# Transposing DMAs in place of TensorE transposes for the rows of the expert blocks

## The chip, the cores and the metric

The kernel runs on one core of a Trainium2 chip. The metric is the device time of one execution in microseconds (us); lower is better. Engine names follow the profile: PE is TensorE (matrix products and transposes; PEld is its loading of weights), DVE is VectorE, ACT is ScalarE, POOL is GpSimd, SP is SyncE, which computes nothing and issues most of the DMAs. SPq is the queue of instructions of SyncE that issue DMAs.

## The reference

Two layers follow each other. The first is sparse attention over 4 batches with 8 heads, 768 positions and 64 elements per head: keys lie in chunks of 32, each query keeps the six chunks with the highest upper bound of its score, and softmax attention runs over these. Its output, seen as 3072 tokens of 512 elements, goes into a mixture of experts with a dense branch:

```
h_dense = np.maximum(x @ w1_dense, 0.0)
y_dense = h_dense @ w2_dense
logits = x @ w_gate
expert_idx = np.argmax(logits, axis=1)
...
    h = np.maximum(x[mask] @ w1[e], 0.0)
    y_moe[mask] = gate_w[mask, None] * (h @ w2[e])
return (y_dense + y_moe).astype(np.float32)
```

There are 8 experts, each with two 512 by 512 matrices; a token goes to one expert only. `gate_w` is the softmax weight of that expert.

## The kernel before, in words

**Attention, and the dense branch beside it.** The kernel works through 16 pairs of heads (four pairs per batch). While it works on the attention of one batch, the dense branch of the batch before is put in as filler: transposes of x (L257), the gate (L265 to L282), the dense products (L383, L392) and the stores of the dense result (L398, through SyncE's queue, two stores of 64 rows for each 128 tokens).

**The table.** Each token's attention output, in half precision, is kept as one row of 512 elements with 32 further 16-bit words, of which the first two are the gate weight (a float) and the next two the token's number (an integer). When the expert of a token is known, GpSimd scatters its row into `table` in device memory (L368), in which each expert has a range of rows. A row is 544 words of 16 bits, 1088 bytes. So the rows of one expert lie one behind the other, and a block is 128 such rows.

**The blocks.** There are at most 31 blocks of 128 rows; 28 run always, and the last three only if they are needed, behind a branch. The numbers of first row and of expert of each block are calculated on DVE and read into registers (L430). The first 11 blocks (`N1`) hold only tokens of the first three batches, and can be fetched while the last batch is still in its attention. The other 17 have to wait until the last batch's rows are in the table; the rows behind each expert's last token are filled with an empty pattern by eight DMAs (`empty`, L728 in the profile), which also precede them.

**One block.** `fetch(i)` (L448 to L452) puts one plain DMA into SyncE's queue, which brings the 128 rows into the tile `xg`, 128 partitions by 544 words. `tx(i)` transposes the 512 elements on TensorE, in four pieces of 128 by 128, into PSUM (L684), and DVE copies the result to `exT` (L686). `e1(i)` multiplies by the expert's first matrix (L692, four matmuls of 512 columns), ACT applies the relu (L695, tile `eh`). `th(i)` transposes this on TensorE (L701), ACT copies it to `ehT` (L703). `e2(i)` multiplies by the second matrix (L709), DVE multiplies by the gate weight, which is read from `xg` (L712, tile `yo`, four buffers), and GpSimd scatters the result into the output with an adding DMA (L713), by the token numbers, which are also read from `xg`.

**Order.** Each engine runs its instructions in the order in which they were put in its queue. The loop at the end puts, for each i, e1(i), tx(i+1), some pieces of the last batch's gate and dense branch in the first iterations, e2(i-1) and th(i). The loop puts in fetches up to 8 blocks ahead (`AHEAD`); the first six (`FIRST`) are put in already during the last pair of heads. A framework orders the queues by priority and adds the waits. `xg` has 14 buffers, so a fetch waits for a buffer only from the 15th block on. The DMAs of SyncE's queue use eight semaphores in turn, and each DMA waits for the one that used the same semaphore before, so that at most eight are under way.

Of the kernel before, what the change touches and what calls it, by code (L numbers as in the profile page):

```python
# [8 lines left out]
FP = mybir.dt.float32  # L9
BF = mybir.dt.bfloat16  # L10
HF = mybir.dt.float16
AF = mybir.ActivationFunctionType
ALU = mybir.AluOpType
# [4 lines left out]
def kernel(  # L18
# [12 lines left out]
    nc = tc.nc  # L31
# [3 lines left out]
    N, Dm = out.shape  # L35
    E = 8
    F = 512
    NK = Dm // 128
# [5 lines left out]
    XW = Dm + 32  # L44
    U16 = mybir.dt.uint16
# [8 lines left out]
    table = dram.tile([EMPTY + 128, XW], U16, name="table")  # L54
# [17 lines left out]
    eg = ctx.enter_context(tc.tile_pool(name="eg", bufs=14))  # L72
# [25 lines left out]
    ident = const.tile([128, 128], HF)  # L98
# [142 lines left out]
    def apart(dma, group, reason):  # L241

        if group in groups:
            tc.declare_no_dep(dma.ins, group=group, reason=reason)
        groups.add(group)
        tc.add_to_no_dep_group(group, dma.ins)
# [179 lines left out]
    offs = []  # L426
    rows = []
# [7 lines left out]
    def load_offs():  # L435

        k = len(offs)
        n, c = (min(4, N1 - k), k) if k < N1 else (min(4, NBLK - k), k - N1 + N1R)
        offs.extend(registers(eo[:, c : c + n], mybir.EngineType.PE, (E - 1) * 2 * NK * 512,
                              "the expert of a block is at most the last"))  # L440

    def load_rows(n):
        rows.extend(registers(ro[:, len(rows) : n], mybir.EngineType.SP, EMPTY,
                              "blocks lie in their expert's rows, or are the empty one"))

    es = [dict() for _ in range(NBLK)]

    def fetch(i):  # L448
        es[i]["x"] = xg = eg.tile([128, XW], U16, name="xg")
        ld = nc.sync.dma_start(out=xg, in_=table[bass.ds(rows[i], 128)])  # L450
        if i < N1:
            tc.add_to_no_dep_group("full", ld.ins)  # L452

    FIRST = 6
    with (
# [167 lines left out]
        for i, (p, u) in enumerate(seq):  # L623
# [37 lines left out]
            if p == NP - 1 and 3 <= u < 3 + FIRST:  # L661
                fetch(u - 3)
# [5 lines left out]
    with (  # L668
        tc.tile_pool(name="p1", bufs=2, space=bass.MemoryType.PSUM) as p1,
        tc.tile_pool(name="p2", bufs=2, space=bass.MemoryType.PSUM) as p2,  # L670
        tc.tile_pool(name="p3", bufs=2, space=bass.MemoryType.PSUM) as p3,
        tc.tile_pool(name="p4", bufs=1, space=bass.MemoryType.PSUM) as p4,
        tc.tile_pool(name="et", bufs=2) as et,
    ):
        cur.update(tr=(p1, "tr"), h=(p2, "h"), y=(p3, "y"), rk=(p4, "rk"))
        assert not fills
        a, d, ranks, places, _ = batch_fills(B - 1)

        wef = we.rearrange("p e j f -> p (e j f)")
        def tx(i):  # L680
            s = es[i]
            tp = p1.tile([128, NK, 128], HF, name="tp", tag="tr")
            for ko in range(NK):
                nc.tensor.transpose(tp[:, ko], s["x"][:, ko * 128 : (ko + 1) * 128].bitcast(HF), ident)  # L684
            s["xT"] = xT = et.tile([128, NK, 128], HF, name="exT")
            nc.vector.tensor_copy(xT, tp)  # L686

        def e1(i):
            s = es[i]
            hp = p2.tile([128, 512], FP, name="hp", tag="h")  # L690
            for ko in range(NK):
                nc.tensor.matmul(hp, s["xT"][:, ko], wef[:, bass.ds(offs[i] + ko * 512, 512)],  # L692
                                 start=(ko == 0), stop=(ko == NK - 1))
            s["h"] = h = et.tile([128, 512], HF, name="eh")
            nc.scalar.activation(h, hp, AF.Relu)  # L695

        def th(i):
            s = es[i]
            tp = p1.tile([128, NK, 128], HF, name="tp", tag="tr")
            for j in range(NK):  # L700
                nc.tensor.transpose(tp[:, j], s["h"][:, j * 128 : (j + 1) * 128], ident)  # L701
            s["hT"] = hT = et.tile([128, NK, 128], HF, name="ehT")
            nc.scalar.copy(hT, tp)  # L703

        def e2(i):
            s = es[i]
            yp = p3.tile([128, Dm], FP, name="yp", tag="y")
            for j in range(NK):
                nc.tensor.matmul(yp, s["hT"][:, j], wef[:, bass.ds(offs[i] + (NK + j) * 512, 512)],  # L709
                                 start=(j == 0), stop=(j == NK - 1))  # L710
            o = et.tile([128, Dm], FP, name="yo", bufs=4)
            nc.vector.tensor_scalar(o, yp, s["x"][:, Dm : Dm + 2].bitcast(FP), None, ALU.mult)  # L712
            sc = nc.gpsimd.indirect_dma_start(  # L713
                out=out, out_offset=bass.IndirectOffsetOnAxis(ap=s["x"][:, Dm + 2 : Dm + 4].bitcast(mybir.dt.int32), axis=0),
                in_=o, in_offset=None, bounds_check=N - 1, oob_is_err=False, compute_op=ALU.add)
            latest["pool"] = sc
            apart(sc, "add", "every token is in one block")
            if i < N1:
                tc.declare_no_dep(sc.ins, group="dense", reason="the first blocks hold no token of the last batch")
                tc.add_to_no_dep_group("add1", sc.ins)  # L720

        def empty():

            _, at_ = nc.values_load_multi_w_load_instructions(
                zo, engines=[mybir.EngineType.SP], min_val=0, max_val=EMPTY - 128,
                skip_runtime_bounds_check_because="an expert has room for all tokens and a block more")
            for e in range(E):
                z = nc.sync.dma_start(out=table[bass.ds(at_[e], 128)], in_=zt)  # L728
                apart(z, "rows", "these rows are no token's")
                tc.declare_no_dep(z.ins, group="full", reason="the first blocks end before these rows")  # L730

        AHEAD = 8
        READY = 4
        tx(0)
        extra = {0: a[:NT] + [a[NT], ranks], 1: places[:2], 2: places[2:4], 3: places[4:] + [empty]}
        for n, f in enumerate(d):
            extra.setdefault(1 + n * (N1 - 2) // len(d), []).append(f)
        got = FIRST

        RARE = 3  # L740
        NOFT = NBLK - RARE
        for i in range(NOFT):
            if i == READY:
                load_rows(NBLK)
            while got < min(i + AHEAD + 1, NOFT if i >= READY else N1):
                fetch(got)
                got += 1
            e1(i)
            if i + 1 < NOFT:
                tx(i + 1)  # L750
            for f in extra.get(i, ()):
                f()
            if i > 0:
                e2(i - 1)
            if len(offs) < min(i + 4, NBLK):
                load_offs()
            if i == READY + 1:
                total = nc.values_load(nblk, min_val=0, max_val=N2,  # L758
                                       skip_runtime_bounds_check_because="the blocks that are left are at most N2")
            th(i)  # L760
        e2(NOFT - 1)
        with tc.If(total > N2 - RARE):
            for i in range(NOFT, NBLK):
                fetch(i)
                tx(i)
                e1(i)
                th(i)
                e2(i)
# [30 lines left out]
```

## Time and profile before

| | |
|---|---|
| Median of the runs | 259.3 us (259.21 and 259.4) |
| The profiled execution | 258.3 us, its span 256.5 us |
| PE busy | 213.9 us (83%), 2547 instructions |
| DVE, ACT, POOL busy | 181.2, 177.7, 161.5 us |
| Transposes of x (L684) | 112, 219 ns each |
| Copies to exT (L686) | 28, 425 ns each |
| Row fetches (L450 in SyncE's queue) | 28, 136 KB each, 338 ns of the queue each (median) |
| Scatters into the output (L713) | 28, 1554 ns of POOL each, 5.1 us to landing |
| First and last scatter into the output start | 182.5 and 249.6 us |

The span is the time from the first to the last instruction of the profiled execution, and the execution's own time is a little longer. Busy time of an engine counts neither the issue of DMAs from SyncE nor waits. In the timeline, a line has the start in us from the beginning of the span, the duration (from the first to the last of a group where several are put together), engine, line, operation, the tile written and the tiles read, the number of instructions, and in brackets how long the engine was idle before it and what ended that. The expert loop runs from 173 us to the end; before it, nothing is touched by the change.

### The profile page before, as it was taken

Reading aid. Unit: us, or ns where it says so; the run is one execution under the profiler, and the core shown is the slowest. Engines: PE = TensorE matmul, PEld = TensorE weight load, DVE = VectorE, ACT = ScalarE, POOL = GpSimd, SP = SyncE. Lnnn points to the kernel's source line nnn. Section 1 sums busy time; section 2 is a strip of 40 time slices with the busy share of each in tenths; the row PEclk is TensorE's granted clock in tenths of the full one; section 3 lists DMA queues with packets and bytes.
Section 4 is the critical chain, followed back from the end, with each engine's and each line's share of the span. In section 5 each row is a group of like instructions: output and inputs, shape, how many; then the busy total and the mean of one; then the engine's idle time right before and its main releaser. Section 6 shows DMA issues by size and latency. Waiting matters only on the chain. (4 is left out here: it accounts for less than half of the span.)

```text
span 256.5 us, 7304 instructions
## 1 busy us (share of the span) xinstructions
PE 213.9 (83%) x2547; PEld 142.2 (55%) x2547; DVE 181.2 (71%) x622; ACT 177.7 (69%) x331; POOL 161.5 (63%) x197
## 2 busy tenths in 40 slices
PE   0379787787899798899996989979999999999960
PEld 0256565575666576656664766646555555555520
DVE  6878899999968699985799997236633345455440
ACT  2689897887679888878897777964556455555430
POOL 3756988766468575867866553520787462888771
PEclk9999999999999999999999999999999999999995
DMA  7999999999749989999999894366398999688875
GB/s 181 263 265 254 209 252 235 247 224 213 199 107 225 252 204 212 202 290 171 279 230 247 140 181 125 87 169 176 98 301 133 242 277 240 113 138 107 112 105 76
DMA packets 75109, 49.89 MB, mean 195 GB/s; under 512 B 29632, under 2 KB 68160, under 8 KB 75072
## 3 DMA queue, kind: packets, MB, share of 16 engines
q1 hardware_dynamic: 59856, 30.33, 46.5%
q0 software_dynamic: 15216, 19.09, 45.4%
q8 instruction: 21, 0.34, 0.6%
q14 instruction: 16, 0.13, 0.1%
HBM read 41.66 MB, written 18.23 MB: 234 GB/s over the span
## 5 line engine op out<-in xcount | busy, mean ns | idle before, releaser
L551 ACT ACTIVATE ex<-sp 128x512 f16<-128x512 f32 (+1 forms) x176 | 92.4, 593 | 10.8 <-PE sp L547 10.6
L547 PE MATMUL sp<-rT,kT 128*128 128x128 f16 (+3 forms) x384 | 63.0, 262 | 2.4 <-ACT ex L551 0.8
L553 POOL TENSOR_SCALAR_AFFINE_SELECT ex<-ex 128x512 f16<-128x512 f16 x48 | 33.2, 699 | 37.6 <-ACT ex L551 37.5
L713 POOL DMA_INDIRECT out_dram<-yo,xg x28 | 43.7, 1561 | 20.2 <-DVE yo L712 12.1
L566 PE MATMUL op<-v,ex 128*128 128x65 f16 x672 | 48.7, 194 | 4.3 <-POOL ex L553 2.8
L566 PEld LDWEIGHTS <-ex 128*128 128x128 f16 x672 | 37.0, 98 | 17.7 <-POOL ex L553 6.2
L712 DVE TENSOR_SCALAR yo<-yp,xg 128x512 f32<-128x512 f32 x28 | 21.0, 750 | 24.9 <-PE yp L709 17.1
L368 POOL DMA_INDIRECT table<-xbig,slot x24 | 24.4, 1019 | 19.1 <-DVE nf L324 11.3
L547 PEld LDWEIGHTS <-kT 128*128 128x128 f16 x384 | 28.3, 98 | 6.7 <-issue 4.2
L703 ACT COPY ehT<-tp 128x512 f16<-128x512 f16 x28 | 16.4, 585 | 19.8 <-PE tp L701 19.8
L692 PE MATMUL hp<-we,exT 128*128 x112 | 29.1, 379 | 1.1 <-DVE xbig L577 1.1
L709 PE MATMUL yp<-we,ehT 128*128 x112 | 28.7, 379 | 0.8 <-ACT ehT L703 0.8
L383 PE MATMUL hp<-xT,wd 128*128 128x384 f16 x128 | 26.2, 325 | 1.7 <-ACT hT L385 1.1
L392 PE MATMUL yp<-wd,hT 128*128 128x512 f16 x96 | 24.4, 378 | 1.0 <-ACT ys L395 0.4
L695 ACT ACTIVATE eh<-hp 128x512 f16<-128x512 f32 x28 | 16.7, 598 | 11.5 <-PE hp L692 10.9
L395 ACT COPY ys<-yp 128x512 f32<-128x512 f32 x24 | 14.2, 593 | 10.2 <-PE yp L392 6.6
L490 DVE TENSOR_TENSOR k<-kp 128x384 f16<-128x384 f16 x32 | 13.8, 469 | 9.9 <-ACT kp L483 9.8
L385 ACT ACTIVATE hT<-hp 128x384 f16<-128x384 f32 x32 | 15.9, 496 | 6.6 <-PE hp L383 6.3
L686 DVE COPY exT<-tp 128x512 f16<-128x512 f16 x28 | 11.8, 423 | 11.5 <-PE tp L684 10.5
L483 ACT COPY kp<-pp 128x768 f16<-128x768 f16 x16 | 12.9, 804 | 7.9 <-PE pp L481 7.9
L577 DVE TENSOR_TENSOR xbig<-op,rs 128x384 f16<-128x384 f32 x32 | 17.6, 550 | 0.4
L475 POOL CAST v<-vf 128x768 f16<-128x768 f32 x16 | 13.9, 871 | 5.0 <-DMA vf<-in_v_dram 3.0
(124 smaller groups left out, 403.0 us busy)
## 6 DMA issues: line engine op xcount, KB each, us to landing
we<-in_moe_w_dram POOLq DMA_DIRECT2D x16, 512.0 KB, 8.2
kf<-in_k_dram SPq DMA_DIRECT2D x32, 192.0 KB
qf<-in_q_dram SPq DMA_DIRECT2D x32, 192.0 KB
vf<-in_v_dram SPq DMA_DIRECT2D x32, 192.0 KB
out_dram<-ys SPq DMA_DIRECT2D x48, 128.0 KB
xg<-table SPq DMA_DIRECT2D x28, 136.0 KB
table<-zt SPq DMA_DIRECT2D x9, 136.0 KB
wd<-in_moe_w_dense_dram POOLq DMA_DIRECT2D x2, 512.0 KB, 6.3
```

Source lines behind the costliest of these rows:

```text
L368: sc = nc.gpsimd.indirect_dma_start(out=table, out_offset=bass.IndirectOffsetOnAxis(ap=keep["slot"][:, t : t + 1], axis=0), in_=xbig[b % 2 ...
L383: nc.tensor.matmul(hp, wd[:, ko, j * 128 : (j + 1) * 128], xT[:, ko, g * G * 128 : (g + 1) * G * 128], start=(ko == 0), stop=(ko == NK - 1))
L392: nc.tensor.matmul(yp, hold["h"][:, j, i * 128 : (i + 1) * 128], wd[:, NK + j], start=(j == 0), stop=(j == NK - 1))
L547: nc.tensor.matmul(sp[:, o : o + w], kT[p % NB][g][:, kt * 128 : (kt + 1) * 128], rT[p % NB][g][:, a * 128 : z * 128], start=(o == 0), sto ...
L551: nc.scalar.activation(ex[:, 0:o], sp[:, 0:o], AF.Exp, scale=-0.125)
L553: latest["pool"] = nc.gpsimd.affine_select(out=ex, in_=ex, compare_op=ALU.is_ge, fill=0.0, base=0, pattern=[[0, 4], [1, 2], [2, 64]], chan ...
L566: nc.tensor.matmul(s["op", g][:, t * (D + 1) : (t + 1) * (D + 1)], ex[:, o : o + 128], v16[p % NB][:, g, kt, :], start=first, stop=(last_o ...
L577: nc.vector.tensor_tensor(xbig[b % 2][:, :, h0 : h0 + D], opv[:, :, 0:D], rs.to_broadcast([128, NT, D]), ALU.mult)
L692: nc.tensor.matmul(hp, s["xT"][:, ko], wef[:, bass.ds(offs[i] + ko * 512, 512)], start=(ko == 0), stop=(ko == NK - 1))
L709: nc.tensor.matmul(yp, s["hT"][:, j], wef[:, bass.ds(offs[i] + (NK + j) * 512, 512)], start=(j == 0), stop=(j == NK - 1))
L712: nc.vector.tensor_scalar(o, yp, s["x"][:, Dm : Dm + 2].bitcast(FP), None, ALU.mult)
L713: sc = nc.gpsimd.indirect_dma_start(out=out, out_offset=bass.IndirectOffsetOnAxis(ap=s["x"][:, Dm + 2 : Dm + 4].bitcast(mybir.dt.int32), a ...
```

## The change

The rows are no longer fetched whole. For each block one plain DMA brings only the last 32 words of each row (gate weight, token number), 64 bytes, into a smaller `xg`, and four transposing DMAs, each of 128 rows by 128 columns, bring the 512 elements straight into `exT`, already transposed. `exT` is now a tile of the pool `eg` with 14 buffers. All five go through SyncE's queue. The function `tx` with its TensorE transposes and its DVE copy is gone, and so are its three calls. DVE and GpSimd find gate weight and token number at another place of `xg`.

```diff
     def fetch(i):
-        es[i]["x"] = xg = eg.tile([128, XW], U16, name="xg")
-        ld = nc.sync.dma_start(out=xg, in_=table[bass.ds(rows[i], 128)])
+        es[i]["x"] = xg = eg.tile([128, XW - Dm], U16, name="xg")
+        es[i]["xT"] = xT = eg.tile([128, NK, 128], U16, name="exT")
+        lds = [nc.sync.dma_start(out=xg, in_=table[bass.ds(rows[i], 128), Dm:XW])]
+        for ko in range(NK):
+            lds.append(nc.sync.dma_start_transpose(out=xT[:, ko], in_=table[bass.ds(rows[i], 128), ko * 128 : (ko + 1) * 128]))
         if i < N1:
-            tc.add_to_no_dep_group("full", ld.ins)
+            for ld in lds:
+                tc.add_to_no_dep_group("full", ld.ins)
...
-        def tx(i):
-            s = es[i]
-            tp = p1.tile([128, NK, 128], HF, name="tp", tag="tr")
-            for ko in range(NK):
-                nc.tensor.transpose(tp[:, ko], s["x"][:, ko * 128 : (ko + 1) * 128].bitcast(HF), ident)
-            s["xT"] = xT = et.tile([128, NK, 128], HF, name="exT")
-            nc.vector.tensor_copy(xT, tp)
-
         def e1(i):
...
-                nc.tensor.matmul(hp, s["xT"][:, ko], wef[:, bass.ds(offs[i] + ko * 512, 512)],
+                nc.tensor.matmul(hp, s["xT"][:, ko].bitcast(HF), wef[:, bass.ds(offs[i] + ko * 512, 512)],
                                  start=(ko == 0), stop=(ko == NK - 1))
...
-            nc.vector.tensor_scalar(o, yp, s["x"][:, Dm : Dm + 2].bitcast(FP), None, ALU.mult)
+            nc.vector.tensor_scalar(o, yp, s["x"][:, 0:2].bitcast(FP), None, ALU.mult)
             sc = nc.gpsimd.indirect_dma_start(
-                out=out, out_offset=bass.IndirectOffsetOnAxis(ap=s["x"][:, Dm + 2 : Dm + 4].bitcast(mybir.dt.int32), axis=0),
+                out=out, out_offset=bass.IndirectOffsetOnAxis(ap=s["x"][:, 2:4].bitcast(mybir.dt.int32), axis=0),
                 in_=o, in_offset=None, bounds_check=N - 1, oob_is_err=False, compute_op=ALU.add)
...
-        tx(0)
...
             e1(i)
-            if i + 1 < NOFT:
-                tx(i + 1)
...
                 fetch(i)
-                tx(i)
                 e1(i)
```

## The prediction

> **What bounds the kernel now.** I read the end of the kernel first, since the change touches nothing before 166.9 us, and went from the engines' busy shares by stage to one iteration of the expert loop, and then to the queue that feeds it.
>
> Busy time by stage (columns: stretch, its length, then for each engine busy us and instructions in brackets, granted clock, share of the 16 DMA engines, GB/s):
>
> ```profile
> core 0: us, PE busy (x) PEld busy (x) DVE busy (x) ACT busy (x) POOL busy (x), PEclk, DMA share, GB/s
> 197.00:209.00 12.00, 11.89 (x80) 6.31 (x78) 4.54 (x8) 6.78 (x12) 5.77 (x4) 1.00 1.06 249
> 209.00:229.00 20.00, 20.00 (x150) 11.23 (x148) 10.44 (x18) 10.77 (x19) 12.85 (x9) 1.00 0.84 172
> 229.00:245.00 16.00, 15.65 (x114) 8.52 (x113) 8.75 (x15) 8.39 (x15) 12.47 (x9) 1.00 0.83 117
> ```
>
> TensorE is busy throughout, while DVE and ACT are half idle. The DMA engines are close behind (0.83 to 1.06). One iteration in the timeline (start, duration, what):
>
> ```profile
> 219.70 0.39 PE L701 MATMUL tp<-ident,eh 128*128 128x128 f16 x4
> 219.93 1.03 PE L692 MATMUL hp<-we,exT 128*128 x4
> 220.06 1.55 POOL L713 DMA_INDIRECT out_dram<-yo,xg  x1 [0.30 <-issue]
> 220.79 0.39 PE L684 MATMUL tp<-ident,xg 128*128 128x128 f16 x4
> 221.01 1.03 PE L709 MATMUL yp<-we,ehT 128*128 x4
> 221.05 0.60 ACT L695 ACTIVATE eh<-hp 128x512 f16<-128x512 f32 x1 [0.28 <-PE hp L692]
> ```
>
> From one start to the next on TensorE: transposes of h 0.23 us (219.70 to 219.93), first matmuls 0.86, transposes of x 0.22 (220.79 to 221.01), second matmuls about 0.87; 2.18 us in all. So TensorE sets the period, and GpSimd is next: a scatter of 1.55 plus 0.30, 1.85 us. Now SyncE's queue, which issues all row fetches (a group's start, time from the first start to the last end, number):
>
> ```profile
> 166.94 1.44 SPq L450 DMA_DIRECT2D xg<-table  x3
> ...
> 173.17 3.56 SPq L450 DMA_DIRECT2D xg<-table  x6
> ...
> 196.69 0.94 SPq L450 DMA_DIRECT2D xg<-table  x2
> 197.74 3.44 SPq L398 DMA_DIRECT2D out_dram<-ys  x4
> ```
>
> One fetch instruction lasts 0.338 us (median of 28), but the distance between starts is longer, as register work and the address stand between: (1.44 - 0.34)/2 = 0.55, (3.56 - 0.34)/5 = 0.64, 0.94 - 0.34 = 0.60. No wait is recorded in the last two groups. I take **0.60 us of SyncE's queue per fetch**, 0.26 of it not the instruction itself. With one fetch per block and a block each 2.18 us the queue runs far ahead. That is the slack which the change spends.
>
> [...] The trace shows 219 ns for one on TensorE when four follow each other; no run here shows the DMA one. [...]
>
> **The change part by part.**
>
> *Removed.* 112 transposes and 28 copies (L684, L686). On TensorE 28 x 0.22 = 6.2 us, at most, and only where TensorE sets the pace: 17 blocks of the part after 209 us, 3.7 us. What becomes late next: h of one block (eh, 0.28 + 0.60 us after the first matmuls) was hidden behind the transposes of x and the second matmuls (0.22 + 0.87) and has only the latter now, so 0.05 us of the 0.22 may come back, and then GpSimd's 1.85 binds. The copies on DVE (28 x 0.42 = 11.8 us) are worth nothing by themselves: DVE is half idle beside TensorE.
>
> *Moved operands and tile sizes.* The gate and the token number come from a 64-byte row instead of the 1088-byte one: the same DVE and GpSimd instructions with another address, nothing. Both tiles have 14 buffers, as xg had, so prefetch depth stays.
>
> *Added.* Each block needs one plain fetch and four transposing ones on the one SyncE queue, 140 DMAs for 28. Price of a transposing one: [...] 0.47, plus the 0.26 between instructions: **0.73 us**. Bounds: 0.34 to 0.36 below, if the interspersed register work overlaps[...]. A gain from the issue itself is excluded: five instructions replace one. A block then costs the queue 0.60 + 4 x 0.73 = **3.52 us**, against 2.18 us that TensorE needs. SyncE becomes the bound. Nothing hides this: prefetch distance buys time once, not rate.
>
> *Sum along SyncE's queue*, with the instructions in its issue order. It starts at 166.94, when the rows of the first three batches lie in the table (the queue waits for GpSimd's scatters there, 6.1 us in the waits).
> 1. First 11 blocks: 11 x 3.52 = 38.7. Between them six stores of the dense layer at 0.60 (2.40 for four at 168.48), 3.6; one register load 0.54 and one zero fill 0.60: 1.1. End 210.3. The consumer wants block 10 at 209.0 (its matmuls follow block 9's of 206.88) and gets it a little late.
> 2. Seven zero fills (4.36 for seven), two stores 1.2, register load 0.5: 216.4. The later fetches must see these fills landed (2.4 us is the shortest landing that the table shows): about 217.
> 3. Remaining 17 blocks: 17 x 3.52 = 59.8, and ten stores, 5.8: 282.7. GpSimd's table scatters of the last batch (the last at 190.1) have long landed, so even a few us of delay there is covered.
> 4. Landing, 2.4: 285.1. From the last block's first matmul (244.50) to the end of the span (256.5) it is 12.0 now; the same instructions follow: 297.1.
>
> Behind a waiting SyncE stand the dense stores (their buffers ys are three, and ACT waits for them) and the zero fills; both are counted in the same queue. TensorE is in order: its first matmuls of blocks 0 and 1 stand ahead of the last batch's gate. Block 1 would land at 166.9 + 7.0 + 1.2 + 2.4 = 177.5 instead of being used at 174.4, so the routing of the last batch slips by some 3 us; the scatter at 190 becomes 193 and step 2 at 217 covers it.
>
> The profiled execution took 258.3 us with a span of 256.5, so 1.8 lie around it: 298.9. The median shown is 259.3, 1.0 above: **300 us**, 16% slower.
>
> **The rivals.**
> 1. [...] 11 blocks end at 235.8, the middle 242.6, 17 more and ten stores 347.7, plus 14.4 and 2.8: 365. [...] A milder version lies between: the DMA engines are already busy 0.83 with scatters, and 512 rows of 256 bytes per block displace them; eight DMAs of this queue are in flight at most, so a landing beyond 5.8 us would also exceed 0.73 us each (scatters land in 4.3 to 6.5).
> 2. *The fetches are hidden* (not slower). Place: SyncE's queue after 197 us. If five DMAs take less than 2.2 us, 0.44 each, TensorE keeps its pace, loses the 0.22 and meets GpSimd's 1.85: 17 x 0.2 = 3.4 us less, 256 us. It decides from 0.44 us each downwards; against it, no unwaited group above shows plain ones under 0.55.
> 3. *Transposing costs the queue no more than a plain fetch*, 0.60: 3.0 per block. Steps: 204.6, 211.4, 268.2, plus 17.2: 285. At 0.55 for all: 278. It is the near end of my forecast.
>
> **How the numbers follow.** Forecast with its near end (0.55 to 0.95 us each, 278 to 325): 0.62. [...] (325 to 365): 0.26. Hidden, or nearly: 0.12, of which 0.03 faster by over 2%, 0.05 within 2%, 0.04 a little slower. Two per cent (5.2 us) is about what a measurement of this kernel can tell from no change. Range 275 to 350: it leaves out the hidden case[...]. Slower by over 2%: 0.92.
>
> **What would show it.** In the changed profile: L684 and L686 gone; SyncE's DMA instructions on exT nearly back to back from 167 us to about 280, starts 0.73 apart; TensorE waiting for exT's DMAs after 210 us, its busy share there near 1.9/3.5; GpSimd's scatters 3.5 us apart with idle time that ends at DVE's yo. Rival 1 shows as waits of SyncE on its own earlier DMAs and starts 1.3 apart; rival 2 as a TensorE period under 2.1 us. I am wrong if the transposing instructions take under 0.3 us of the queue, or if landing times, not the issue, set their distance.

## The result and the profile after

The changed kernel takes 365.8 us (two runs: 365.19 and 366.43) against 259.3 us: a ratio of 1.412, 95% interval 1.399 to 1.424. The forecast was slower, at 300 us, with a range that ended at 350. The sign and the place were right, the size was not: the loss is 106.5 us where 41 were forecast. The profiled execution took 365.19 us with a span of 363.2 us (before: 258.3 and 256.5).

First the tile of the transposed rows in the changed kernel (minimum, median and maximum of one instruction in ns, then the first and last start; below, how long in us, and how often, TensorE stood idle until one of these DMAs, how that divides between weight loads and matmuls, and the time from issue to landing):

```profile
L453 SPq DMA_TRANSPOSE exT<-table x112: 1093/1141/2151, 166.9 to 348.7; - x112
...
  DMA exT<-table: 125.4, 93
...
  PEld L688: 71.2, 53
  PE hp L688: 54.2, 40
...
DMA to landing us min/median/max: 2.2/2.3/6.1
```

One transposing DMA keeps SyncE's queue for 1.14 us, where the forecast took 0.47, the author's estimate for an instruction that no trace of before had shown. For what these DMAs bring, the matmuls of TensorE stood 54.2 us and its weight loads 71.2 us; the two run beside each other (busy 238.9 and 142.8 us in a span of 363.2), so their sum, 125.4, is not time lost by TensorE. The landing, 2.3 us, is what the forecast had (2.4).

Next SyncE's queue in the changed kernel, in the form in which the prediction showed it (a group's start, its time from the first start to the last end, the number of instructions):

```profile
246.20 0.36 SPq L451 DMA_DIRECT2D xg<-table  x1
246.70 4.97 SPq L453 DMA_TRANSPOSE exT<-table  x4
251.89 0.41 SPq L451 DMA_DIRECT2D xg<-table  x1
252.44 4.92 SPq L453 DMA_TRANSPOSE exT<-table  x4
257.46 2.46 SPq L398 DMA_DIRECT2D out_dram<-ys  x4
260.11 0.44 SPq L451 DMA_DIRECT2D xg<-table  x1
...
291.80 1.17 SPq L398 DMA_DIRECT2D out_dram<-ys  x2
...
332.16 17.73 SPq L453 DMA_TRANSPOSE exT<-table  x14
350.14 1.54 SPq L451 DMA_DIRECT2D xg<-table  x3
```

The distance between transposing DMAs is (4.97 - 1.14)/3 = 1.28 us, and over the fourteen in a row (17.73 - 1.14)/13 = 1.28. A block takes 251.89 - 246.20 = 5.69 us of the queue; the forecast had 3.52. The queue is full from 246.2 to 351.7: 17 x 5.69 + 10 stores at 0.6 = 102.7 of 105.5 us. SyncE waits for others only 4.4 us in that stretch, in six waits, so the time is in the instruction itself and not in a wait before it.

One block on TensorE in the changed kernel (timeline; in brackets the idle time before, and what ended it):

```profile
289.14 0.59 PE L688 MATMUL hp<-we,exT 128*128 x1 [1.83 <-DMA exT<-table]
290.44 0.58 PE L688 MATMUL hp<-we,exT 128*128 x1 [0.71 <-DMA exT<-table]
291.71 0.59 PE L688 MATMUL hp<-we,exT 128*128 x1 [0.69 <-DMA exT<-table]
292.93 0.58 PE L688 MATMUL hp<-we,exT 128*128 x1 [0.64 <-DMA exT<-table]
...
293.31 1.91 PE L705 MATMUL yp<-we,ehT 128*128 x4
```

The four matmuls that stood together (1.03 us for four) now start 1.27 us apart, each as its own 128 x 128 piece lands. That is the queue's distance, seen at the consumer.

Last the busy time by stage in the changed kernel, with the columns of before:

```profile
core 0: us, PE busy (x) PEld busy (x) DVE busy (x) ACT busy (x) POOL busy (x), PEclk, DMA share, GB/s
240.00:280.00 40.00, 19.96 (x92) 8.38 (x91) 5.25 (x7) 9.80 (x17) 6.23 (x4) 0.74 0.41 73
280.00:320.00 40.00, 20.92 (x70) 7.75 (x70) 4.50 (x6) 6.54 (x12) 14.00 (x9) 0.69 0.52 80
320.00:350.00 30.00, 17.13 (x70) 6.80 (x67) 3.75 (x5) 7.10 (x12) 7.77 (x5) 0.79 0.45 62
```

TensorE is busy 50 to 57% of the time, the other compute engines less, and the DMA engines 0.41 to 0.52 (0.83 and more before). No engine is the bound. The queue that issues is.

### The profile page after: what moved, and what is told of

The parts are those of the page before. It is cut to its first block, busy times and chain, and to the rows that moved or that the text cites. A ratio compares the mean times of both kernels' runs of the same rounds, so it can differ in the third digit from the quotient of the medians.

```text
span 363.2 us, 7293 instructions
## 1 busy us (share of the span) xinstructions
PE 238.9 (66%) x2435; PEld 142.8 (39%) x2435; DVE 170.3 (47%) x594; ACT 177.6 (49%) x331; POOL 161.5 (44%) x197
## 5 line engine op out<-in xcount | busy, mean ns | idle before, releaser
L688 PE MATMUL hp<-we,exT 128*128 x112 | 42.2, 444 | 55.5 <-DMA exT<-table 54.2
L705 PE MATMUL yp<-we,ehT 128*128 x112 | 36.7, 459 | 14.9 <-ACT ys L395 14.0
L570 PEld LDWEIGHTS <-ex 128*128 128x128 f16 x672 | 36.9, 98 | 17.6 <-POOL ex L557 6.1
L688 PEld LDWEIGHTS <-exT 128*128 128x128 f16 x112 | 11.2, 104 | 75.5 <-DMA exT<-table 71.2
L392 PE MATMUL yp<-wd,hT 128*128 128x512 f16 x96 | 28.5, 427 | 14.4 <-ACT ys L395 13.9
L395 ACT COPY ys<-yp 128x512 f32<-128x512 f32 x24 | 14.2, 593 | 42.3 <-DMA out_dram<-ys 33.7
L383 PE MATMUL hp<-xT,wd 128*128 128x384 f16 x128 | 28.3, 347 | 1.7 <-ACT hT L385 1.1
L705 PEld LDWEIGHTS <-ehT 128*128 128x128 f16 x112 | 12.4, 112 | 31.8 <-issue 23.2
L392 PEld LDWEIGHTS <-hT 128*128 128x128 f16 x96 | 9.7, 105 | 25.2 <-issue 20.2
```

What stands on the lines that cost most here:

```text
L383: nc.tensor.matmul(hp, wd[:, ko, j * 128 : (j + 1) * 128], xT[:, ko, g * G * 128 : (g + 1) * G * 128], start=(ko == 0), stop=(ko == NK - 1))
L392: nc.tensor.matmul(yp, hold["h"][:, j, i * 128 : (i + 1) * 128], wd[:, NK + j], start=(j == 0), stop=(j == NK - 1))
L570: nc.tensor.matmul(s["op", g][:, t * (D + 1) : (t + 1) * (D + 1)], ex[:, o : o + 128], v16[p % NB][:, g, kt, :], start=first, stop=(last_o ...
L688: nc.tensor.matmul(hp, s["xT"][:, ko].bitcast(HF), wef[:, bass.ds(offs[i] + ko * 512, 512)], start=(ko == 0), stop=(ko == NK - 1))
```

## The experiments

Each kernel ran beside the kernel before on the same chip. Those medians of before lay between 258.6 and 265.0 us, so what is compared from chip to chip is the ratio. The kernels with four plain DMAs, with one DMA and with two pieces ran twice each, on one chip; their differences, 6 to 16%, are far above the spread of the kernel before there (257.6 to 261.6).

### Is it the number of DMAs, or that they transpose?

The first kernel keeps the four DMAs but makes them plain; the matmuls then read x untransposed, so the transposition is left out.

```diff
-            lds.append(nc.sync.dma_start_transpose(out=xT[:, ko], in_=table[bass.ds(rows[i], 128), ko * 128 : (ko + 1) * 128]))
+            lds.append(nc.sync.dma_start(out=xT[:, ko], in_=table[bass.ds(rows[i], 128), ko * 128 : (ko + 1) * 128]))
```

> The four fetches of 128 by 128 stay four DMAs of the same shape and order, but plain ones, so the expert products get x untransposed (the output is not the reference's). Theory A, it is the transposing: a transposing DMA holds SyncE's queue for 1.14 us where a plain one holds it for 0.37, starts fall from 1.27 to about 0.60 apart, a block costs the queue 3.0 us and the time is about 285 us. Theory B, it is the number of DMAs (five per block, eight in flight, their landing): the time stays within 10 us of 366 us.

Measured: 287.44 us, ratio 1.113 (1.106 to 1.120). The tile, and a block of SyncE's queue, of the kernel with four plain DMAs:

```profile
L453 SPq DMA_DIRECT2D exT<-table x112: 328/333/2267, 167.2 to 268.4; - x112
```

```profile
246.01 0.33 SPq L451 DMA_DIRECT2D xg<-table  x1
246.59 1.92 SPq L453 DMA_DIRECT2D exT<-table  x4
248.77 0.33 SPq L451 DMA_DIRECT2D xg<-table  x1
```

The instruction takes 0.333 us, the distance is (1.92 - 0.33)/3 = 0.53, and a block takes 248.77 - 246.01 = 2.76. Five instructions instead of one cost 29 us, even when they are plain. That they transpose costs the other 78 or so of the loss. Rival 3 of the prediction, the same sum with 0.60 us for each, gave 285. That this is so near is in part luck: with the 2.76 us that a block really takes, the same sum gives 279, so 8 us are lost that it does not count, most of them before the 12th block's fetch: it starts at 214.0 us, where the sum has 208.7.

### Per instruction, or per byte?

The second kernel fetches a block with one transposing DMA of 128 x 512.

```diff
-        for ko in range(NK):
-            lds.append(nc.sync.dma_start_transpose(out=xT[:, ko], in_=table[bass.ds(rows[i], 128), ko * 128 : (ko + 1) * 128]))
+        lds.append(nc.sync.dma_start_transpose(out=xT, in_=table[bass.ds(rows[i], 128), 0:Dm]))
```

> One transposing DMA of 128 by 512 per block in place of four of 128 by 128; the result is the same. Theory A1, the price is per instruction: the instruction lasts about 1.2 us of the queue, a block costs the queue 2.0 us, the fetches are hidden and the time is 255 to 262 us. Theory A2, the price goes by the amount transposed: the instruction lasts 4 x 1.14 = 4.6 us, only three gaps of 0.13 us per block go, and the time is about 356 us.

Measured: 275.0 us, ratio 1.065 (1.057 to 1.072). The tile of this kernel:

```profile
L452 SPq DMA_TRANSPOSE exT<-table x28: 1189/1200/3168, 167.2 to 248.1; - x28
...
DMA to landing us min/median/max: 2.6/2.8/7.7
```

Four times as much costs 1.20 us of the queue instead of 1.14. Between these two sizes the price is one of the instruction, with 0.02 us for each further 128 x 128. It lands 0.5 us later. This settles rival 1, by which the DMAs' own work and not their issue sets the pace: if each 128 x 128 took the 1.28 us that lie between two of them in the change, such a block would need 5.1 us, and it lands 2.8 us after its issue. Yet neither expectation had 275: the queue now needs only 2.00 us per block, no more than TensorE, and 16 us are lost all the same. That remainder is taken up below.

The third kernel fetches two of the four pieces and uses each twice, so half of x is left out.

```diff
-        for ko in range(NK):
+        for ko in range(NK // 2):
...
-                nc.tensor.matmul(hp, s["xT"][:, ko].bitcast(HF), wef[:, bass.ds(offs[i] + ko * 512, 512)],
+                nc.tensor.matmul(hp, s["xT"][:, ko % 2].bitcast(HF), wef[:, bass.ds(offs[i] + ko * 512, 512)],
```

> Only the first two of the four pieces are fetched, and used twice in the product (half of x is left out). If each transposing DMA costs the queue its 1.27 us and nothing else binds, 56 x 1.27 = 71 us go and the time is about 295 us, with a block at 0.6 + 2.5 = 3.1 us of the queue. If the end is set by something that does not go by their number (a landing, the order of the queue), well above 310 us.

Measured: 298.62 us, ratio 1.156 (1.149 to 1.164). Each instruction still takes 1.13 us. The 56 instructions that are gone were worth 67 us, 1.20 each.

A last suspicion was the row number, which SyncE reads from a register. In this kernel the transposing DMAs read constant rows, so x is not the tokens' own.

```diff
-            lds.append(nc.sync.dma_start_transpose(out=xT[:, ko], in_=table[bass.ds(rows[i], 128), ko * 128 : (ko + 1) * 128]))
+            lds.append(nc.sync.dma_start_transpose(out=xT[:, ko], in_=table[EMPTY : EMPTY + 128, ko * 128 : (ko + 1) * 128]))
```

> The changed kernel with all transposing DMAs reading the same constant rows of the table in place of the block's own (so the expert products get other tokens' data). If the 1.14 us of SyncE's queue are the transposing instruction's own, they stay and the time is 360 to 368 us. If they come from the address in a register, the instruction falls to about 0.5 us and the time to about 280 us.

Measured, in one run: 367.17 us beside a kernel before of 263.3 us. The tile of this kernel:

```profile
L453 SPq DMA_TRANSPOSE exT<-table x112: 1099/1230/3153, 169.5 to 350.2; - x112
```

The instruction did not become shorter, so the price is not that of the address.

### What was the removed work worth?

This is the kernel before without its transposes of x on TensorE and the copies on DVE. The matmuls read x untransposed (left out: the transposition), and no DMA is added.

```diff
     def tx(i):
         s = es[i]
-        tp = p1.tile([128, NK, 128], HF, name="tp", tag="tr")
-        for ko in range(NK):
-            nc.tensor.transpose(tp[:, ko], s["x"][:, ko * 128 : (ko + 1) * 128].bitcast(HF), ident)
-        s["xT"] = xT = et.tile([128, NK, 128], HF, name="exT")
-        nc.vector.tensor_copy(xT, tp)
+        s["xT"] = s["x"][:, 0:Dm].rearrange("p (k c) -> p k c", k=NK).bitcast(HF)
```

> The kernel before with TensorE's transposes of x and DVE's copies left out: the product reads the fetched rows as they are, so x is not transposed. This is what the change removes, alone. By the prediction 17 blocks after 209 us win 0.2 us each until GpSimd's 1.85 us binds: 3.4 us, about 256 us. If TensorE's whole 6.2 us count: 253 us. If the scatters already set the end: 259 us, no change.

Measured: 257.4 us (20 runs), ratio 0.995 (0.993 to 0.998): 1.2 us where the prediction had 17 x 0.2 = 3.4. The timeline of this kernel shows where the rest stays:

```profile
219.11 1.56 POOL L709 DMA_INDIRECT out_dram<-yo,xg  x1 [4.16 <-DMA xg<-table]
...
219.87 1.02 PE L705 MATMUL yp<-we,ehT 128*128 x4
...
220.66 0.28 PEld L697 LDWEIGHTS <-eh 128*128 128x128 f16 x4 [0.26 <-ACT eh L691]
...
220.98 1.55 POOL L709 DMA_INDIRECT out_dram<-yo,xg  x1 [0.30 <-issue]
...
221.84 0.62 PEld L705 LDWEIGHTS <-ehT 128*128 128x128 f16 x4 [0.36 <-ACT ehT L699]
221.93 1.02 PE L705 MATMUL yp<-we,ehT 128*128 x4
...
222.84 1.55 POOL L709 DMA_INDIRECT out_dram<-yo,xg  x1 [0.30 <-issue]
...
249.29 1.55 POOL L709 DMA_INDIRECT out_dram<-yo,xg  x1 [0.51 <-DVE yo L708]
```

TensorE now waits for ACT twice per block, 0.26 and 0.36 us, so its period is 2.06 us (219.87 to 221.93) where the kernel before has 2.18: 0.12 of the 0.22 are won. GpSimd's scatters follow each other 1.86 us apart, 1.55 each and 0.30 between. They are catching up after a wait, which the next part deals with, and that takes them almost to the end: after the first of them at 219.11, sixteen more at 1.86 would put the last at 248.9, and it starts at 249.29. So with this order of the rest, a still shorter period of TensorE would win only 0.4 us more, and no form of the change, however cheap its DMAs, should gain much over half a per cent. Another order was not tried.

### What is left with one DMA per block?

With one DMA of 128 x 512 the queue is as fast as TensorE, and 16 us are still lost. Theory Q: the in-order SyncE queue delays what stands behind the fetches, the last batch's dense stores above all. Theory D: the transposing DMAs load the DMA engines.

A scatter of a block that holds tokens of the last batch adds to rows that the dense stores have written, so it must follow the last of them. The scatters of the kernel before and of the kernel with one DMA per block, from the last one free of this to the end (timeline of GpSimd):

```profile
212.42 1.57 POOL L713 DMA_INDIRECT out_dram<-yo,xg  x1 [0.81 <-DVE yo L712]
218.19 1.56 POOL L713 DMA_INDIRECT out_dram<-yo,xg  x1 [4.20 <-DMA xg<-table]
...
249.64 1.55 POOL L713 DMA_INDIRECT out_dram<-yo,xg  x1 [0.51 <-DVE yo L712]
```

```profile
226.02 1.57 POOL L708 DMA_INDIRECT out_dram<-yo,xg  x1 [0.76 <-DVE yo L707]
235.39 1.56 POOL L708 DMA_INDIRECT out_dram<-yo,xg  x1 [7.80 <-DMA exT<-table]
...
266.57 1.55 POOL L708 DMA_INDIRECT out_dram<-yo,xg  x1 [0.51 <-DVE yo L707]
```

That the late scatters wait for the stores is in the kernel's dependencies; the profile names as releaser only the DMA that it took to be last. The last dense store was issued shortly before in both (211.84 and 227.82). The DMA packets that the traces hold confirm it: the last of these stores' packets (2048 bytes, a row of the result) ended at 216.99 and 233.86 us, 1.2 and 1.5 us before the scatter, and in the change at 294.39, 1.4 us before it (295.76). Set side by side, in us later than in the kernel before (first late scatter 218.19, last 249.64, span 256.5; the chip of the three experiments is like the first one's, 258.6 against 259.3):

| kernel | last dense store issued | first late scatter | last scatter | span |
|---|---|---|---|---|
| one DMA of 128 x 512 | +16.0 | +17.2 | +16.9 | +17.0 |
| two pieces | +43.5 | +41.0 | +40.5 | +40.4 |
| four plain | +27.2 | +24.8 | +29.9 | +29.2 |
| the change | +80.0 | +77.6 | +107.1 | +106.7 |

With one DMA or two pieces the whole loss is there before the first late scatter, and from it to the end of the span it takes 38.1 and 37.7 us, as before (38.3). So after it the transposing DMAs do not slow the scatters. With four plain DMAs another 5 us come later, and in the change another 29.5. So SyncE's queue costs twice: once through the rate of the fetches, once through the place of the stores behind them.

The first attempt at Q moved the last batch's dense stores to ACT's queue, in the kernel with one DMA and, as a control, in the kernel before.

```diff
-                    st_ = nc.sync.dma_start(out=outv[m, j], in_=ys[64 * j : 64 * j + 64])
+                    st_ = (nc.scalar if b == B - 1 else nc.sync).dma_start(out=outv[m, j], in_=ys[64 * j : 64 * j + 64])
```

> One transposing DMA per block as in the run with one of 128 by 512, and the last batch's twelve dense stores are issued by ACT in place of SyncE. Theory Q, what that run still loses (275 us) is a wait: its dense stores stand behind fetches, fills and a register load in SyncE's queue, ACT waits 15 us for their buffers and TensorE for ACT; without that, 256 to 260 us. Theory D, the transposes load the DMA engines (about 47% of them by SyncE's DMAs from 215 to 255 us) and slow the scatters: 268 us or more, with DVE waiting for scatters.

> The kernel before with only these twelve stores on ACT, as the control. In it ACT waits 1.9 us for these buffers after 195 us, so by theory Q it gains at most that: 257 to 259 us. If issuing on ACT by itself is worth more (or costs ACT time in the loop), it shows here.

Measured: 278.9 us, ratio 1.061 (1.052 to 1.070), and for the control 264.45 us, ratio 1.003 (1.001 to 1.006). No gain, and no verdict on Q: the stores did not come free of a queue. The last of them was issued at 228.84 us, no earlier than from SyncE (227.82), and ACT stood still in between. The timeline of the kernel with one DMA and stores on ACT:

```profile
198.56 0.59 ACT L698 COPY ehT<-tp 128x512 f16<-128x512 f16 x1 [10.47 <-DMA out_dram<-ys]
```

The second attempt left the stores where they are and gave the last batch's ys its own six buffers, since ACT waited for these stores 15.2 us in all (two waits) in the kernel with one DMA. The same edit was put into the kernel before and into the change.

```diff
-                ys = my.tile([128, Dm], FP, name="ys")
+                ys = cur.get("ys", my).tile([128, Dm], FP, name="ys")
...
+        tc.tile_pool(name="myl", bufs=6) as myl,
     ):
...
+        cur["ys"] = myl
```

> One transposing DMA per block as in the run with one of 128 by 512, and the last batch's six dense results have a buffer each, so that ACT need not wait for their stores in SyncE's queue. Theory Q (what is left of the loss there is ACT, and TensorE behind it, waiting for those buffers): ACT's 15 us of waits go and the time falls from 275 to 257 to 263 us. Theory D (the transposes slow the DMA engines, and with them the scatters and the fills): 268 us or more, DVE waiting for scatters.

> The kernel before with the same six buffers, as the control: ACT waits 1.9 us for them there, so 0 to 2 us less than the kernel before.

> The changed kernel (four transposing DMAs per block) with the same six buffers. If the sum of SyncE's queue sets its end, the queue's content is the same and the time stays at 363 to 368 us, though ACT's 33 us of waits for stores go. If those waits are part of the loss, 335 to 350 us.

Measured: one DMA 274.37 us, ratio 1.037 (1.033 to 1.041); before 265.12 us, ratio 1.000 (0.997 to 1.003); the change 371.22 us, ratio 1.403 (1.396 to 1.409). The first wins back nearly half of its loss (1.065 to 1.037), yet falls short of what Q forecast: by its number it lies on D's side. ACT's waits for the stores are gone from its trace, so what failed is Q's claim that these waits were the whole of the remainder. The other two do not move. In the change the waits for buffers are thus no part of the loss. What is left with one DMA is the gate again: the copies into the tile of the dense results (first and last start at the end of the line), then the timelines of SyncE and GpSimd, of the kernel with one DMA and own buffers:

```profile
L395 ACT COPY ys<-yp x24: 585/585/687, 72.2 to 208.6; 128x512 f32<-128x512 f32 x24
...
229.72 1.16 SPq L398 DMA_DIRECT2D out_dram<-ys  x2
...
233.74 1.56 POOL L710 DMA_INDIRECT out_dram<-yo,xg  x1 [12.62 <-DMA xg<-table]
```

The last of the copies (L395) ended at 208.6 + 0.6 = 209.2 us, and the stores of its tile were issued 20.5 us later, behind seven further fetches in SyncE's queue. In the kernel before it ended at 206.6, and they were issued 5.3 us later. The first late scatter starts 8.3 us later than in the kernel before with the same buffers (225.41, in an execution 1.3 us above its median), which is most of the 9.7 us lost.

Two more kernels tried to tell Q from D. One prefetches three blocks ahead instead of eight, so that fewer fetches stand ahead of the stores:

```diff
-        AHEAD = 8
+        AHEAD = 3
```

> The run with one transposing DMA per block and own buffers for the dense results, with fetches at most 3 blocks ahead in place of 8, so that the fills, the register load and the dense stores stand earlier in SyncE's queue. In the run before it, the scatter of the first block of the last batch waited 12.6 us (4.2 in the kernel before), as the last dense store was issued at 229.7 us (211.8) behind eight fetches. If the place of these stores in the queue is what is left of the loss (274.4 us beside 264.6 on that chip), they move to before 215 us and the time is within 3 us of the kernel before's on the same chip. If the transposes' load on the DMA engines is it, it stays 8 to 10 us above.

Measured: 274.9 us, ratio 1.035 (1.030 to 1.041), no change, which by its number is again D's side. Its one profile (278.1 us, longer than its median) shows that the test missed its aim: TensorE now waited for rows, the last dense result came 11.5 us later (its copy at 220.1 instead of 208.6), and its stores, issued only 4 us earlier (225.81), ended no sooner with their last packet (232.54, formerly 232.32). The other leaves the queue its instructions and takes away three quarters of the transposed bytes: the one DMA brings 128 columns, which are used four times (left out: three quarters of x).

```diff
-        for ko in range(NK):
+        for ko in range(1):
...
-                nc.tensor.matmul(hp, s["xT"][:, ko].bitcast(HF), wef[:, bass.ds(offs[i] + ko * 512, 512)],
+                nc.tensor.matmul(hp, s["xT"][:, 0].bitcast(HF), wef[:, bass.ds(offs[i] + ko * 512, 512)],
```

> As the run with one DMA of 128 by 512 and own buffers (1.0367 of the kernel before), but the one transposing DMA per block brings only the first 128 columns, which the product uses four times (three quarters of x are left out). SyncE's queue has the same instructions, at 1.14 in place of 1.20 us; the transposed bytes fall to a quarter. If what is left of the loss is the queue's order and time, the ratio stays at 1.03 to 1.04. If it is the load of the transposes on the DMA engines, it falls to 1.00 to 1.01.

Measured: 281.29 us, ratio 1.069 (1.061 to 1.077). That is neither theory's number: Q had 1.03 to 1.04, D 1.00 to 1.01. Its copies of the dense results and its timelines of SyncE and GpSimd have the gate once more, later still:

```profile
L395 ACT COPY ys<-yp x24: 585/585/687, 72.0 to 210.7; 128x512 f32<-128x512 f32 x24
...
238.38 1.12 SPq L398 DMA_DIRECT2D out_dram<-ys  x2
...
242.28 1.56 POOL L711 DMA_INDIRECT out_dram<-yo,xg  x1 [23.81 <-DMA exT<-table]
```

The queue had nearly the same instructions, but not in the same order: 13 transposing DMAs stand between the fills and the last dense store, where the kernel with 128 x 512 has seven. The stores were issued 27.1 us after their result was ready (211.3). This leaves little room for D: with a quarter of the bytes the stores take as long from their issue to their last packet (2.6 us in both), and from the first late scatter to the end it is 36.9 us instead of 39.0, so about 2 of the 9.7 us can be the bytes'.

So the traces of all versions put the remainder down to the stores' place in SyncE's queue. No run moved the stores forward and left the rest as it was, so this is read from the traces and not shown by an experiment, and why the framework's order puts the last store there stays open. It bears on 4 to 7% in versions with one DMA, not on the 41% of the change.

## Why the prediction was right and wrong

*The step that failed* is the price in "Added": 0.47 us for a transposing instruction, 0.73 with what lies between. Measured are 1.14 and 1.28; what lies between is 0.14, not 0.26, so the whole error is in the instruction. The mechanism is the forecast's own (SyncE's queue becomes the bound and TensorE waits for exT), and its sum stands for the change: with 5.7 us per block the first 11 blocks end at 166.9 + 62.7 + 4.7 = 234.3 (measured 236.1), the fills, stores and landing bring 240.9 (measured: the next fetch at 246.2), 17 blocks and ten stores 343.6, and with 14.4 and 2.8 it gives 361, beside 365.8 measured. The other 5 us are the first step (+1.8), the middle one (+3.5, the next fetch started 6.0 us after the last fill was issued), the third (105.5 instead of 102.7, +2.8) and the end (11.5 us after the last issue instead of 14.4, -2.9). Where the queue is not full the sum fails: with 2.00 us per block, as in the kernel with one DMA, it gives 257, and 275 was measured.

*Where the wrong price came from.* The 0.47 was the author's estimate, since no trace of before held a transposing DMA. It is 1.39 times the 0.338 us that the trace did show, for a plain one of the same queue; the runs have 1.14/0.333 = 3.4 times. The prediction gave 0.26 to times of 325 to 365, but for another reason, that of rival 1. What the runs show is a time of the issuing queue: 128 x 512 takes 1.20 us, not four times 1.14.

*The range.* The prediction's own slowest case was 365 us, and its range stopped at 350. No trace had shown the operation, so none spoke for leaving that end out.

*Rival 1* (365) hit the time by its number, not by its reason. It expected starts 1.3 apart, which are there (1.28), and waits of SyncE for its own DMAs, which are not: none of the six waits from 246.2 to 351.7 us, 4.4 us in all, is put down to one. The DMA engines are half idle (0.41 to 0.52). Its milder version, eight DMAs in flight at most, does not show either: at 1.28 us apart and 2.3 us landing, about two are in flight. *Rival 2* (hidden) needed under 0.44 us each and is refuted even for plain ones (0.53). *Rival 3* (285) is near what four plain DMAs measure (287), with a price that is too high (0.60 instead of 0.53) in place of waits that it left out.

*The signs.* TensorE's share was to be near 1.9/3.5 = 0.54, and 0.50 to 0.57 are there; but this is luck, since a block takes 5.7 us and not 3.5, and each matmul lasts longer (0.59 us, where four took 1.03).

*Removed.* Forecast 3.7 us at most for the 17 late blocks, of which 0.05 per block might come back; measured 1.2. More comes back than was thought (0.10 of 0.22, in TensorE's waits for ACT), and GpSimd's 1.86 us was named correctly as the next bound.

*Cover.* "Nothing hides this" was right. Routing of the last batch was to slip by 3 us and slipped by 14: its last scatter into the table starts at 204.4 us, formerly at 190.1. The fills, which end at 240.2, cover that too. The dense stores were counted in the queue as so many times 0.60 us, but not as a gate: the first late scatter, 4.0 us after the last of them was issued, came 77.6 us later in the change. The sum could do without it, because the last fetch ends later still; for two pieces or one DMA it could not. The scatters were forecast 3.5 us apart; instead they come in trains at 1.86 us with long gaps before them.

## What to carry to other kernels

Price a transposing DMA by the instruction on the queue that issues it, here 1.14 us for 128 x 128 and 1.20 for 128 x 512, so make it large (one of 128 x 512 in place of four of 128 x 128 took the ratio from 1.412 to 1.065), and multiply by the number per iteration before comparing with the period of the engine that sets the pace. Then list what stands in the same in-order queue behind it, stores and fills that gate another engine above all: that loss stays when the rate is mended (16 us here). And ask first what the removal alone is worth, by leaving the work out: here 0.5%, too little for DMAs that are not free.

## What the runs showed of the hardware that was not expected

- A transposing DMA takes 1.14 us of SyncE's queue for 128 x 128 two-byte elements and 1.20 us for 128 x 512, and the first after SyncE had waited takes no less (1.19 at 166.95 us and 1.16 at 246.70), so it is no backlog. Its landing, 2.3 us, grows by 0.5 us (to 2.8) for 96 KB more; 96 KB in 0.5 us are about 200 GB/s, an estimate for the data alone.
- TensorE's granted clock was lower in the stages in which it starved: 0.69 to 0.79 in the change, against 1.00 in the three stages of before. Four matmuls took 1.91 us instead of 1.03. What this costs was not measured apart.
- With the stores issued from ACT's queue ACT itself stood 10.47 us at one point, until a dense store had landed.
- By the packets in the traces, the last dense stores took 2.6 us from issue to last packet in the change, with two pieces and with own buffers, where few scatters were under way, and 5.2 us in the kernel before and 6.0 with one DMA, where packets of the scatters took 55 of 82 and 60 of 97 us of the DMA engines' time.
